# Norm rows summed on DVE before the matmul that reduces them, and activation tables loaded ahead of use

## The chip, the cores and the metric

One NeuronCore of a Trainium2 chip runs the whole program. The metric is the device time of one execution in microseconds (us). Most executions agree within 0.3%. All runs told here are fast (granted TensorE clock 0.998 to 1.0). The engines are PE (matmuls), PEld (its weight loads), DVE (VectorE), ACT (ScalarE), POOL (GpSimd) and SP.

## The reference

Two parts follow each other. Per batch, an attention matrix between channels is made from q and k (6080 rows of 256 channels), with norms over those rows, one per channel; it is applied to v, and the result goes through a two-layer network with a squared ReLU.

```python
qn = q / (np.linalg.norm(q, axis=1, keepdims=True) + 1e-06)
kn = k / (np.linalg.norm(k, axis=1, keepdims=True) + 1e-06)
s = kn.transpose(0, 2, 1) @ qn / tau
s = s - s.max(-1, keepdims=True)
a = np.exp(s)
a /= a.sum(-1, keepdims=True) + 1e-09
x = v @ a                         # 4 batches x 6080 rows x 256
h = x @ w_in                      # 256 -> 2048
r = np.maximum(h, 0.0)
out = (s_moe * (r * r) + b_moe) @ w_out
```

## The kernel before

The kernel walks through 48 groups of 512 tokens (the last has 256), 16 steps each. A step issues two h_ps matmuls and, of the group before, 7 of the 112 small matmuls that make the output from seven products p1 to p7 (a Strassen-like scheme; DVE forms the sums S1 to S4 for it). The products share PSUM tiles, and DVE evicts each one before the next may write there:

```python
products = [
    ("X", G(0, 0), W[:, 0, :, lo], p1),       # evicted to u1
    ("Z", lambda: S[1], T1, p5),              # evicted to u5
    ("X", lambda: S[2], T2, p6),              # waits for u1
    ("Y", G(1, 0), W[:, 1, :, lo], p2),       # Y shares a tile with Z: waits for u5
    ("X", lambda: S[3], T3, p7),
    ("Z", lambda: S[4], W[:, 1, :, hi], p3),
    ("X", G(1, 1), N4, p4),                   # waits for p7's eviction
]                                             # (comments added)
```

Batches 1, 2 and 3 are prepared beside this stream. Their rows come in 12 chunks; per chunk, PE adds to the Gram matrix (s_ps), DVE squares q and ACT squares k, and DVE folds four rows of squares into one row of 2 x 256 (two arrays, q and k). These rows were kept, and reduced over the partitions at the end by matmuls with a column of ones, in a burst:

```python
def fold(half, arrays, last):
    ...
        if last:
            self.rows.append((st["f", half], np_, 1))
...
def add_norms(self, last=False):
    ...
    self.n_ps = x_tile[0][:, 1, : 2 * CH].rearrange("p (a c) -> p a c", a=2)   # unused half of X's tile
    for i, (t, np_, j, a, ch) in enumerate(todo):
        po(nc.tensor.matmul(self.n_ps[:, a, ch : ch + 1], t[:np_, a, j, ts(ch, P)], ones16[:np_, 0:1], ...))

def norms():
    self.add_norms(last=True)
    nrm = sm_pool.tile([P, 2, CH], FP32, tag="nrm", name="nrm")
    po(nc.scalar.activation(out=nrm, in_=self.n_ps, func=AF.Sqrt))
```

The scheduling of a later batch, by steps (cut):

```python
w0 = first_group[b - 1] * FT + (26 if b == 1 else 6)
w1 = first_group[b] * FT - 3
fin_len = 54                       # lead of the finish over the first use
span = (w1 - fin_len) - w0 - 8     # steps over which the chunks are spread
...
for i, f in enumerate(gr.norm_ops(c)):
    at_step(int(sc) + 2 + 1 + i * 3, f)
```

In these traces each engine runs its instructions in the order in which the kernel issues them.

Of the kernel before, what the change touches and what calls it, by code (L numbers as in the profile page):

```python
# [11 lines left out]
AF = mybir.ActivationFunctionType  # L12
# [4 lines left out]
def kernel(  # L17
# [12 lines left out]
    nc = tc.nc  # L30
# [23 lines left out]
    def po(ins):  # L54

        tc.keep_in_program_order(ins)
        return ins
# [30 lines left out]
    def h_tile(name):  # L88
        return ps_h.tile([P, 2, TG], FP32, tag="h_ps", name=name)
# [19 lines left out]
    class Gram:  # L109
# [41 lines left out]
        def norm_ops(self, c):  # L151

            qc, kc = self.tiles[c]
            _, np_, jc = self.chunks[c]
            st = {}

            def squares(a, js):
                def f():
                    if "sq" not in st:
                        st["sq"] = sq_pool.tile([P, 2, JC, C], FP16, tag="sq", name="sq")  # L160
                    if a == 0:
                        po(nc.vector.tensor_mul(  # L162
                            st["sq"][:np_, 0, js, :], qc[:np_, js, :], qc[:np_, js, :]))
                    else:
                        po(nc.scalar.activation(  # L165
                            out=st["sq"][:np_, 1, js, :], in_=kc[:np_, js, :], func=AF.Square))
                return f

            def fold(half, arrays, last):
                def f():  # L170
                    src = st["f", 2 * half] if 2 * half < jc else st["sq"]
                    if ("f", half) not in st:
                        if last:
                            t = f3_pool.tile([P, 2, 1, C], FP16, tag="f3", name="f3")
                        else:
                            t = sq_pool.tile([P, 2, half, C], FP16, tag=f"f{half}", name="f")
                        st["f", half] = t
                    po(nc.vector.tensor_add(  # L178
                        st["f", half][:np_, arrays], src[:np_, arrays, :half, :],
                        src[:np_, arrays, half : 2 * half, :]))  # L180
                    if last:
                        self.rows.append((st["f", half], np_, 1))
                return f

            def unfolded():
                self.rows.append((st["sq"], np_, jc))

            ops = []
            for h in range(0, jc, 4):
                js = slice(h, min(h + 4, jc))  # L190
                ops += [squares(1, js), squares(0, js)]
            if jc == 2:
                return ops + [unfolded]
            if jc == 8:
                ops += [fold(4, slice(0, 1), False), fold(4, slice(1, 2), False)]
            return ops + [fold(2, slice(0, 2), False), fold(1, slice(0, 2), True)]

        def add_norms(self, last=False):

# [15 lines left out]
        def finish_ops(self):  # L215

            st = {}
# [23 lines left out]
                        po(nc.tensor.transpose(  # L241
                            st["t"][:, j, ts(ch, P)], st["s"][:, ch, ts(j, P)], ident32))

            def ready():

                po(nc.scalar.activation(out=warm, in_=ones32[:, 0:1], func=AF.Exp))

            def exps(j):
                if j == 0:
                    st["e"] = sm_pool.tile([P, CH, C], FP16, tag="eT", name="eT")  # L250
                po(nc.scalar.activation(
                    out=st["e"][:, j, :], in_=st["t"][:, j, :], func=AF.Exp,
                    scale=st["r"][:, 0, j : j + 1]))
                if j == 0:
                    self.wa = apool.tile([P, CH, Dff], FP16, tag="wa16", name="wa16")
# [26 lines left out]
            def fold_both(f0, n):  # L282
                def f():

                    two = [self.bank("wa_ps", CH, C)[:, 0, :n], h_tile("wa_ps")[:, 0, :n]]
                    for m in range(CH):
                        fold_mm(f0, n, m, two[m])
                    for m in range(CH):
                        scaled(f0, n, m, two[m])
                return f  # L290
# [8 lines left out]
            if self.b == 0:  # L299

                folds = [fold_both(0, P), fold_both(P, P)]
                folds += [fold_one(2 * P, NW - 2 * P, m) for m in range(CH)]
            else:
                folds = []
            folds += [fold_one(f0, NW, m) for f0 in range(NW if self.b == 0 else 0, Dff, NW)
                      for m in range(CH)]
            return [norms, recip, ready, turn, lambda: exps(0), lambda: exps(1), sums] + folds

        def bank(self, name, a, b):

# [19 lines left out]
    def transpose_v(g):  # L330
        _, nj = group(g)
        v16 = v_tiles.pop(g)
        vT_ps = ps_o.tile([P, CH, TG], FP16, tag="o_ps", name="vT_ps")
        for j in range(nj):
            for ch in range(CH):
                po(nc.tensor.transpose(vT_ps[:, ch, ts(j, P)], v16[:, j, ts(ch, P)], ident16))
        vT = vtpool.tile([P, CH, TG], FP16, tag="vT", name="vT")
        po(nc.vector.tensor_copy(out=vT[:, :, : nj * P], in_=vT_ps[:, :, : nj * P]))
        vT_tiles[g] = vT
# [19 lines left out]
    ones32 = consts.tile([P, P], FP32)  # L359
# [4 lines left out]
    warm = consts.tile([P, 1], FP32)  # L364
# [36 lines left out]
    def keep_busy(n, w, x):  # L401

        idle_ps = h_tile("idle_ps")[:, 0, :]
        for _ in range(n):
            po(nc.tensor.matmul(idle_ps, w, x, start=True, stop=True, skip_group_check=True))

    for c in range(NCH0):
        ops = g0.norm_ops(c)
# [9 lines left out]
            f()  # L418

    fin = g0.finish_ops()  # L420
    fin[0]()
    fin[1]()
    fin[2]()
    keep_busy(5, w_in16[:, 0, :P], w_in16[:, 0, :NW])
    fin[3]()
    transpose_v(0)
    for f in fin[4:11]:
        f()


# [44 lines left out]
    def at_step(s, f):  # L475
        side.setdefault(int(s), []).append(f)


    FIN = (0, 3, 3, 6, 8, 10, 13)
    first_group = [b * N // TG for b in range(B)]  # L480
    for i, f in enumerate(fin[11:]):
        at_step(i // 2 * 4 - 1 + i % 2 if i > 1 else 0, f)
    at_step(14, lambda: po(nc.vector.tensor_scalar_mul(
        out=s_out, in0=s_bc, scalar1=1.0 / (LAM * LAM))))
# [22 lines left out]
    for b in range(1, B):  # L507
        gr = grams[b]
        w0 = first_group[b - 1] * FT + (26 if b == 1 else 6)
        w1 = first_group[b] * FT - 3  # L510
        NCH = len(gr.chunks)
        fin_len = 54
        span = (w1 - fin_len) - w0 - 8
        n = NCH * JC
        for c in range(NCH):
            sc = w0 + span * c * JC / n
            at_step(max(3, sc - 16), lambda gr=gr, c=c: gr.load(c))
            if c == 0:
                at_step(sc, gr.start)
            for j in range(JC):  # L520
                at_step(w0 + span * (c * JC + j) / n, lambda gr=gr, c=c, j=j: gr.mm(c, j))

            def norm_step(gr=gr, c=c, sc=sc):
                ops = gr.norm_ops(c)
                for i, f in enumerate(ops):
                    at_step(int(sc) + 2 + 1 + i * 3, f)
            at_step(sc + 1, norm_step)

        def fin_step(gr=gr, s=w1 - fin_len):
            ops = gr.finish_ops()  # L530
            for i, f in enumerate(ops):
                at_step(int(s) + 1 + (FIN[i] if i < 7 else FIN[6] + 3 + (i - 7) * 3), f)
        at_step(w1 - fin_len, fin_step)


    def segments(g):
# [264 lines left out]
```

## Time and profile before

| | before |
|---|---|
| time, median | 727.7 us (727.43 to 727.76) |
| PE / DVE / ACT busy | 97% / 86% / 75% |
| tiny norm matmuls of batches 1 to 3 | 144, in three bursts of 48 |
| a burst on PE | 1.18 us |
| table load of the square root | 1.28 us, right ahead of it |

Read it from the chain that ended last: it is 89% PE, so PE's issue time and PE's waits decide. The prediction shows those lines and the ones for DVE.

A measure used below: **lost time**. For each matmul I took the time to the start of the next and subtracted the spacing that its width has in an undisturbed stretch of these traces (0.216 us for 512 columns, 0.109 for 256, 0.056 for 128, 0.025 for one); gaps of more than 0.06 us beyond that are added up. (A gap near that limit can fall on either side, so a total is good to about 0.06 us. A time given with a loss is that of the last matmul before the gap.) "Batch 1" runs from the first p1 matmul of group 1 to that of group 8, "batch 2" on to group 20, "batch 3" on to group 32. The chunks of that batch and, except where a run moves it, its finish lie inside. Before, these stretches lasted 106.09, 174.55 and 174.54 us, with 1.16, 0.86 and 0.86 us lost.

### The profile page before, as it was taken

What the parts mean: (1) busy time and instruction counts of PE and PEld (TensorE: products, weight loads), DVE (VectorE), ACT (ScalarE), POOL (GpSimd) and SP (SyncE); (2) the same over time, 40 slices, a digit from 0 to 9 for tenths busy, and PEclk for the clock granted to TensorE, in tenths of its full rate; (3) what the DMA queues carried; (4) which work ended last, traced back from release to release, by engine and by line L of the source; (5) the groups of instructions that cost most, each with busy time, mean ns of one, the idle gap of its engine ahead of it and who ended that gap; (6) DMA issues with size and microseconds to landing.
All of it is one profiled execution on the core that took longest, in us unless ns stands there. A gap on an engine that the chain in (4) does not pass through costs nothing.

```text
span 725.6 us, 17836 instructions
## 1 busy us (share of the span) xinstructions
PE 704.5 (97%) x7618; PEld 509.2 (70%) x7618; DVE 623.6 (86%) x873; ACT 541.5 (75%) x582; POOL 82.4 (11%) x158
## 2 busy tenths in 40 slices
PE   4799999999999999999999999999999999999997
PEld 2556777776777777777677777777668777777776
DVE  4779999988889989988788989998888888888886
ACT  5489877797778777878777778778777777777772
POOL 4522400001111110001010210000000000000000
PEclk9999999999999999999999999999999999999999
DMA  9999993236499754323767685232333333321201
GB/s 237 209 257 143 205 178 75 59 96 125 89 149 163 122 103 89 95 67 76 141 125 127 126 145 126 67 68 65 91 67 78 90 72 73 96 59 51 75 30 75
DMA packets 81600, 79.57 MB, mean 110 GB/s; under 512 B 55696, under 2 KB 56528, under 8 KB 81520
## 3 DMA queue, kind: packets, MB, share of 16 engines
q0 software_dynamic: 21472, 39.46, 32.1%
q1 hardware_dynamic: 59616, 37.64, 20.3%
q8 instruction: 60, 0.98, 0.6%
q10 hardware_dynamic: 432, 1.31, 0.5%
q14 instruction: 20, 0.16, 0.1%
HBM read 78.91 MB, written 24.90 MB: 143 GB/s over the span
## 4 chain that ended last, share of the span: by engine, by line
PE 89%; ACT 4%; DMA 4%; DVE 1%; issue 1%; ACTq 0%; DVEq 0%; POOLq 0%
PE h_ps L566 43%; PE o_ps L710 38%; PE s_ps L142 4%; DMA qk<-in_q_dram 2%; PE wa_ps L278 2%; ACT r L576 2%; DMA raw<-in_q_dram 1%; PE o_ps L614 1%; ACT g L587 1%; ACT sq L165 1%; DVE f L178 0%; ACT L222 0%; PE t_ps L241 0%; ACT T L470 0%; DVE o_sb L594 0%
## 5 line engine op out<-in xcount | busy, mean ns | idle before, releaser
L576 ACT ACTIVATE r<-h_ps 128x1024 f16<-128x1024 f32 (+1 forms) x384 | 387.8, 1013 | 152.3 <-PE h_ps L566 150.7
L566 PE MATMUL h_ps<-vT,wa 128*128 128x512 f16 (+7 forms) x1632 | 451.9, 364 | 0.6 <-ACT r L576 0.4
L710 PEld LDWEIGHTS <-S 128*128 128x128 f16 x2944 | 198.1, 98 | 86.2 <-issue 1.5
L710 PEld LDWEIGHTS <-g 128*128 128x128 f16 x2208 | 155.0, 98 | 74.1
L589 DVE TENSOR_TENSOR g<-r 128x2048 f16<-128x2048 f16 (+2 forms) x154 | 176.4, 1145 | 17.8 <-ACT r L576 17.5
L710 PE MATMUL o_ps<-T,S 128*128 128x128 f16 x2208 | 183.7, 219 | 0.9 <-ACT nrm L222 0.4
L566 PEld LDWEIGHTS <-wa 128*128 128x128 f16 x1632 | 136.1, 98 | 21.6 <-issue 1.0
L710 PE MATMUL o_ps<-w_out,g 128*128 128x128 f16 x1472 | 134.2, 219 | 0.0
L594 DVE SCALAR_TENSOR_TENSOR o_sb<-o_ps,s_out,u 128x256 f32<-128x256 f32 x138 | 66.4, 481 | 51.6 <-PE o_ps L710 49.5
L587 ACT ACTIVATE g<-r 128x1024 f16<-128x1024 f16 x93 | 97.9, 1053 | 0.0
L325 POOL DMA_DIRECT2D v<-in_v_dram x48 | 25.7, 536 | 520.6 <-DMA vT<-v 353.5
L142 PE MATMUL s_ps<-qk 128*128 128x256 f16 (+1 forms) x384 | 69.5, 281 | 14.5 <-ACT qk L133 6.9
L594 DVE SCALAR_TENSOR_TENSOR u<-o_ps,s_out,rowconst 128x256 f32<-128x256 f32 x138 | 65.9, 477 | 2.8 <-PE o_ps L710 1.6
L710 PE MATMUL o_ps<-N,g 128*128 128x128 f16 x736 | 63.5, 219 | 0.0
L710 PE MATMUL o_ps<-w_out,S 128*128 128x128 f16 x736 | 63.4, 219 | 0.0
L165 ACT ACTIVATE sq<-qk 128x1024 f16<-128x1024 f16 (+3 forms) x49 | 50.4, 1033 | 10.6 <-DMA qk<-in_k_dram 7.5
L638 DVE TENSOR_TENSOR S<-S,g 128x2048 f16<-128x2048 f16 (+1 forms) x47 | 56.4, 1201 | 1.3
L636 DVE TENSOR_TENSOR S<-g 128x2048 f16<-128x2048 f16 (+1 forms) x47 | 56.0, 1192 | 0.0
L642 DVE TENSOR_TENSOR S<-g,S 128x2048 f16<-128x2048 f16 x46 | 55.9, 1215 | 0.0
L640 DVE TENSOR_TENSOR S<-g 128x2048 f16<-128x2048 f16 x46 | 55.9, 1214 | 0.0
L142 PEld LDWEIGHTS <-qk 128*128 128x128 f16 (+1 forms) x384 | 32.6, 100 | 19.9 <-DVE qk L132 8.9
L162 DVE TENSOR_TENSOR sq<-qk 128x1024 f16<-128x1024 f16 (+3 forms) x49 | 33.0, 673 | 2.8 <-DMA qk<-in_q_dram 2.8
(68 smaller groups left out, 281.8 us busy)
## 6 DMA issues: line engine op xcount, KB each, us to landing
out_dram<-o_sb SPq DMA_DIRECT2D x46, 512.0 KB, 3.0
v<-in_v_dram POOLq DMA_DIRECT2D x47, 256.0 KB, 3.8
qk<-in_k_dram POOLq DMA_DIRECT2D x42, 256.0 KB, 7.1
qk<-in_q_dram POOLq DMA_DIRECT2D x42, 256.0 KB, 7.8
vT<-v SPq DMA_TRANSPOSE x182, 2.8
w<-in_moe_w_out_dram POOLq DMA_DIRECT2D x4, 512.0 KB, 12.2
raw<-in_q_dram ACTq DMA_DIRECT2D x2, 512.0 KB, 6.5
raw<-in_k_dram SPq DMA_DIRECT2D x2, 512.0 KB, 6.8
```

What stands on the lines that cost most here:

```text
L142: po(nc.tensor.matmul(self.s_ps[:, ch, :], kc[:np_, j, ts(ch, P)], qc[:np_, j, :], start=(c == 0 and j == 0 and ch == 0), stop=(c == len(s ...
L165: po(nc.scalar.activation(out=st["sq"][:np_, 1, js, :], in_=kc[:np_, js, :], func=AF.Square))
L566: po(nc.tensor.matmul(dst, wa[:, ci, ts(m, P)], src, start=(ci == 0), stop=(ci == CH - 1), skip_group_check=True))
L576: po(nc.scalar.activation(out=r16[:, :, i % 2, :n], in_=h_tiles.pop((g, i))[:, :, :n], func=AF.Relu))
L587: po(nc.scalar.activation(out=dst, in_=src, func=AF.Square))
L589: po(nc.vector.tensor_mul(dst, src, src))
L594: po(nc.vector.scalar_tensor_tensor(out=dst, in0=src, scalar=s_out, op0=ALU.mult, in1=add, op1=ALU.add))
L636: po(nc.vector.tensor_add(T[1], A21, A22))
L638: po(nc.vector.tensor_sub(T[2], T[1], A11))
L640: po(nc.vector.tensor_sub(T[3], A11, A21))
L642: po(nc.vector.tensor_sub(T[4], A12, T[2]))
L710: po(nc.tensor.matmul(st[name][:, j, :], a()[:, i, ts(j, P)], w[:, i, :], start=first, stop=last, skip_group_check=True))
```

## The change

The intent is to take most of the tiny matmuls off PE: the rows of chunks 2 to 12 are added onto the first chunk's row on DVE, so that a burst has 4 matmuls. And the square root's table is to be in place when the norms are: a dummy activation loads it 12 steps ahead, as one already did for the exponential.

```diff
-                    if last:
+                    if last and (self.b == 0 or c == 0):
                         self.rows.append((st["f", half], np_, 1))
...
+            def into_first():
+                dst, src = self.rows[0][0][:np_], st["f", 1][:np_]
+                po(nc.vector.tensor_add(dst, dst, src))
...
-            return ops + [fold(2, slice(0, 2), False), fold(1, slice(0, 2), True)]
+            ops += [fold(2, slice(0, 2), False), fold(1, slice(0, 2), True)]
+            return ops + [into_first] if self.b > 0 and c > 0 else ops
...
-            def ready():
-                po(nc.scalar.activation(out=warm, in_=ones32[:, 0:1], func=AF.Exp))
+            def ready(func):
+                po(nc.scalar.activation(out=warm, in_=ones32[:, 0:1], func=func))
...
-            return [norms, recip, ready, turn, ...] + folds
+            return [lambda: ready(AF.Sqrt), norms, recip, lambda: ready(AF.Exp), turn, ...] + folds
...
-    FIN = (0, 3, 3, 6, 8, 10, 13)
+    FIN = (-12, 0, 3, 3, 6, 8, 10, 13)
...
-        span = (w1 - fin_len) - w0 - 8
+        span = (w1 - fin_len) - w0 - 12
```

The last line squeezes the chunks into 81 steps in place of 85 for batch 1, and 117 in place of 121 for the others, as a chunk now has five operations three steps apart.

More of the change, by code (lines that the diff above doesn't have):

```diff
@@ L306, in finish_ops @@
                       for m in range(CH)]
-            return [norms, recip, ready, turn, lambda: exps(0), lambda: exps(1), sums] + folds
+            return [lambda: ready(AF.Sqrt), norms, recip, lambda: ready(AF.Exp), turn, lambda: exps(0), lambda: exps(1), sums] + folds
         def bank(self, name, a, b):
@@ L420 @@
     fin = g0.finish_ops()
-    fin[0]()
     fin[1]()
     fin[2]()
+    fin[3]()
     keep_busy(5, w_in16[:, 0, :P], w_in16[:, 0, :NW])
-    fin[3]()
+    fin[4]()
     transpose_v(0)
-    for f in fin[4:11]:
+    for f in fin[5:12]:
         f()
@@ L476, in at_step @@
         side.setdefault(int(s), []).append(f)
-    FIN = (0, 3, 3, 6, 8, 10, 13)
+    FIN = (-12, 0, 3, 3, 6, 8, 10, 13)
     first_group = [b * N // TG for b in range(B)]
-    for i, f in enumerate(fin[11:]):
+    for i, f in enumerate(fin[12:]):
         at_step(i // 2 * 4 - 1 + i % 2 if i > 1 else 0, f)
@@ L531, in fin_step @@
             for i, f in enumerate(ops):
-                at_step(int(s) + 1 + (FIN[i] if i < 7 else FIN[6] + 3 + (i - 7) * 3), f)
-        at_step(w1 - fin_len, fin_step)
+                at_step(int(s) + 1 + (FIN[i] if i < 8 else FIN[7] + 3 + (i - 8) * 3), f)
+        at_step(w1 - fin_len - 12, fin_step)
     def segments(g):
```

## The prediction

> **What bounds the kernel now.** I read the page first (busy shares, then the chain that ended last), then the instructions of line 211, which the change thins out, then the chain and the timeline around one burst of them, and last the DVE, which gets the new work.
>
> The page's first part and the two summary lines of its chain:
>
> ```profile
> PE 704.5 (97%) x7618; PEld 509.2 (70%) x7618; DVE 623.6 (86%) x873; ACT 541.5 (75%) x582; POOL 82.4 (11%) x158
> PE 89%; ACT 4%; DMA 4%; DVE 1%; issue 1%; ACTq 0%; DVEq 0%; POOLq 0%
> PE h_ps L566 43%; PE o_ps L710 38%; PE s_ps L142 4%; DMA qk<-in_q_dram 2%; PE wa_ps L278 2%; ACT r L576 2%; DMA raw<-in_q_dram 1%; PE o_ps L614 1%; ACT g L587 1%; ACT sq L165 1%; DVE f L178 0%; ACT L222 0%; PE t_ps L241 0%; ACT T L470 0%; DVE o_sb L594 0%
> ```
>
> The kernel is a stream of matmuls: 89% of the chain is PE, and the granted clock is full in all 40 slices. So an instruction taken off PE after the first 36 us shortens the run by its issue time, unless what stands beside it cannot follow. DVE, at 86%, is the engine that might not.
>
> The norms of a later batch (1, 2, 3) are made by one burst of tiny matmuls in the middle of that stream. The chain in order of time around batch 1's burst:
>
> ```profile
> 148.56 0.39 PE o_ps L710 x7
> 148.95 1.18 PE o_ps L211 x48
> 150.13 0.45 PE h_ps L566 x2
> ```
>
> 48 matmuls hold PE for 1.18 us, 24.6 ns each from start to start. The 163 ns that the list of line 211 gives for one is latency, which overlaps. Around batch 2's burst the chain reads
>
> ```profile
> 322.47 1.02 ACT r L576
> 323.49 0.02 issue
> 323.51 1.28 ACT L222
> 324.79 0.01 issue
> 324.80 0.18 ACT nrm L222
> 324.99 0.04 issue
> 325.03 0.55 PE o_ps L710 x7
> ```
>
> Here the end of the burst is not what lets PE go on: the square root waits for its table (1.28 us), and the next product into the same PSUM tile waits for the square root's read. In the timeline the weight stream restarts at 325.03, while the pair of h_ps matmuls before it began at 324.26 and needs 0.43: the restart would have been at 324.69, so 0.34 us are lost. The gap between the same starts is the same in batch 3; batch 1 loses 0.08.
>
> For DVE, the groups that matter, and the busy time in the three stretches in which a later batch's Gram matrix is gathered:
>
> ```profile
> L178 DVE TENSOR_TENSOR f<-f 128x512 f16<-128x512 f16 (+1 forms) x47 | 19.7, 419 | 0.4
> L636 DVE TENSOR_TENSOR S<-g 128x2048 f16<-128x2048 f16 (+1 forms) x47 | 56.0, 1192 | 0.0
> ...
> 66.00:147.00 81.00, 80.55 (x854) 58.69 (x852) 77.53 (x111) 65.18 (x75) 11.76 (x22) 1.00 0.71 135
> 184.00:322.00 138.00, 137.98 (x1516) 100.80 (x1514) 124.20 (x172) 105.02 (x109) 15.92 (x30) 1.00 0.61 114
> 376.00:497.00 121.00, 120.98 (x1330) 89.41 (x1328) 110.42 (x154) 93.01 (x97) 11.67 (x22) 1.00 0.58 113
> ```
>
> The columns after the length are PE, PEld, DVE, ACT, POOL. DVE is busy 95.7% of batch 1's stretch (3.5 us idle) and 90 to 91% of the other two (13.8 and 10.6 us idle).
>
> **What the Trainium skill says.** "TensorE: Matmul & The Clock Gate", section "Wait — 56ns, not 53.3ns?": start-to-start never drops below about 25 ns however small N is. The trace agrees: 24.6 ns at N=1. "VectorE: DVE Perf Modes", section "The perf-mode tier table": a 16-bit tensor_tensor of 2048 elements takes 1224 ns, at most the 2x mode; the trace has 1192 to 1215 for such adds. "ScalarE: Activation LUTs", section "What ACT_TABLE_LOAD costs": about 1283 ns plus a drain of about 1380. The trace has the 1283, but no further 1380 after it: the square root above starts 0.01 us after its table load ends. I use 1.28.
>
> **The change part by part.**
>
> Removed from PE: a later batch has 12 chunks, each leaving one row of 2 arrays x 2 halves, so 48 matmuls with their weight loads. With the rows added onto the first one, 4 remain. 44 x 24.6 ns = 1.08 us a batch, and all of it lies on the path: 3 x 1.08 = 3.24 us. Batch 0 is untouched (the new fold is for b > 0, and its list of operations only shifts its indices by one).
>
> Moved on ACT: the square root's table now comes with a dummy activation 12 steps (about 10 us) earlier; the load of the exponential was already separate. The number of loads stays the same, and 3 dummies of 0.20 us are added. At the new place ACT has room: between 312 and 318 us relus of 1.02 us follow each other at 1.65 us, so 0.62 idle in each period, and the built order puts the load between pairs of relus with no square in the next four. The load and dummy take 1.40 us from start to the next relu (that is what the exponential's took, 153.37 to 154.77), so that relu is about 0.8 us late. By the timeline a relu ends about 0.8 to 1.0 us before PE writes its buffer again, and the exponential's own load stopped no h_ps matmul. I count no loss, 0.1 at most for one batch.
>
> What that frees: after a burst of about 0.1 us, the next X product stands 0.1 + 0.43 us behind the burst's start. The square root now waits only for the relu in front of it on ACT. With batch 2's times that relu ends at 323.49, the root would end at about 323.65, and PE would want the tile at 323.04 + 0.10 + 0.43 = 323.57: a wait of about 0.05 to 0.15 instead of 0.34. I count 0.25 for each of batches 2 and 3 and 0.05 for batch 1: 0.55 us.
>
> Added on DVE: 11 adds a batch of the form 128x512, 33 in all. One lasts 0.42 us, but the next DVE instruction starts 0.33 after it (73.63 to 73.96 in the timeline), so 11 x 0.33 = 3.7 us a batch. In batches 2 and 3 that fits into the idle 13.8 and 10.6 us. In batch 1 it meets 3.5 us of idle time. There the gathering is also squeezed from 85 steps to 81, so the same adds come 5% closer together, which PE partly shares, its Gram matmuls coming closer too. The limit is reached there, so I walked the built order of DVE from one wait for PE to the next. In the before trace each group of 16 steps (about 15 us) has 0.5 to 1.2 us of DVE idle in its last third. The added work is 0.35 (first group), 0.7, 1.6, 0.7 and 0.7 us in the five groups. The lateness at the third output eviction comes out as 0, 0, 0.3, 0.7 and 0.4 us. PE feels that through the first sum S of each group (line 636), whose first matmul starts only 0.06 to 0.8 us after it is ready. In the new order the small adds fall less often right ahead of it, and only the last group comes out short, by about 0.1. I allow 0.3 us for batch 1, as such a walk can miss one of five, and 0.3 for batches 2 and 3 together, for sums that shift by one add and for PE's waits on a relu, which move with the steps.
>
> Sum: 727.7 - 3.24 - 0.55 + 0.3 + 0.3 = 724.5 us, 0.44% faster.
>
> **The rivals.** First, DVE becomes the bound of batch 1. For it: 95.7% busy, 3.7 us to add into 3.5 us of idle, and a first sum that in one group (at 145.8) is ready just when it is used. Against it: idle time at waits for PE shows that DVE is resynchronised each group, and the stretch without Gram work that follows (DVE 86% busy) pays lateness back. Were all idle time unusable, batch 1 would lose up to about 2 us and the time would be 726.5. Second, the moved table load stalls PE instead of the square root: relus late by 0.8 us with 0.8 to 1.0 of slack could cost 0.2 to 0.5 us in each batch, giving 725.5. Third, the burst was hidden anyway: DVE and ACT used it to catch up, so that PE waits elsewhere for what it no longer spends there. For it: the chain passes through DVE for 5.8 us just ahead of batch 1's burst (142.02 to 147.80), so DVE is behind there. Against it: right after the burst the chain is PE alone, and the sums have 0.4 us of slack with no Gram work left. If half the 3.24 were given back the time would be 726.1.
>
> **The range and the chances.** The best case is all of the 3.24 and of the roots' 0.76, with no loss: 723.7, or a little less if the shifted schedule also drops some of the small waits of before (0.17 us four times on a relu in batches 2 and 3). The rivals reach 725.5 to 726.5 each, and two of them together 727. Eight in ten: 723.4 to 726.4. 2% is 14.6 us; nothing in the change reaches that either way, short of a surprise in a state of the chip or a table loaded many more times, and the built order shows no such loads.
>
> **What would show it.** The list of the tiny matmuls should have 12 in place of 144 on o_ps, each burst about 0.1 us in the chain. The square root should start less than 0.2 us after the relu before it with no table load between. The waits for nrm on PE should fall to 0.1 or vanish. DVE busy should rise by 33 x 0.42, to about 637 us (88%), with batch 1's stretch near 99%. PE's waits on S and on relus should stay within half a microsecond of before. It would be wrong if the matmuls after the burst stand apart by waits on DVE (line 642 of the new kernel), or if h_ps matmuls wait for a relu just after the new table load.

## The result, and the profile after

The changed kernel takes 725.05 us (724.96 to 725.23, 4 runs) against 727.62 for the kernel before in the same rounds: 2.57 us or 0.35% less. The ratio given with the run is 0.9965, 95% interval 0.9948 to 0.9982. Such ratios are the mean time of one kernel's fast runs over that of the other's of the same rounds, so not quite the ratio of the medians quoted. The time lies inside the predicted range, 0.55 us above the predicted 724.5.

The page's first part and the engines of its chain, kernel after:

```profile
PE 702.4 (97%) x7486; PEld 506.5 (70%) x7486; DVE 634.1 (88%) x906; ACT 542.4 (75%) x585; POOL 82.8 (11%) x158
...
PE 83%; DVE 9%; DMA 5%; ACT 1%; issue 1%; POOL 1%; ACTq 0%; POOLq 0%
```

132 matmuls are gone from PE, and DVE is 10.5 us busier. DVE now has 9% of the chain, against 1% before. Most of that lies between 60 and 150 us, in and around batch 1's stretch.

The chain around batch 2's burst, kernel after:

```profile
322.91 0.39 PE o_ps L716 x7
323.30 0.08 PE o_ps L217 x4
323.38 0.45 PE h_ps L572 x2
323.83 0.41 PE o_ps L716 x7
```

Before, this was a chain through ACT's table load and square root. Now PE follows on PE: the burst is 0.08 us, and the next X product starts on time. What ACT does there, from its timeline, kernel after:

```profile
322.55 1.02 ACT L582 ACTIVATE r<-h_ps 128x1024 f16<-128x1024 f32 x1
323.45 0.18 ACT L228 ACTIVATE nrm<-o_ps 128x4 f32<-128x4 f32 x1
```

The square root starts 0.90 us after the start of the relu ahead of it, with no table load between, and ends at 323.63, before PE wants the tile at 323.83. PE's waits for nrm are gone from the list of waits.

The group of the new adds among the groups by line, kernel after:

```profile
L188 DVE TENSOR_TENSOR f<-f,f 128x512 f16<-128x512 f16 (+1 forms) x33 | 13.9, 420 | 0.0
```

And the busy time in the same three stretches as before (columns PE, PEld, DVE, ACT, POOL), kernel after:

```profile
66.00:147.00 81.00, 79.74 (x839) 57.84 (x837) 79.88 (x121) 65.33 (x74) 11.72 (x22) 1.00 0.72 131
184.00:322.00 138.00, 137.82 (x1512) 100.59 (x1510) 127.60 (x183) 106.46 (x111) 14.33 (x27) 1.00 0.56 113
376.00:497.00 121.00, 120.82 (x1323) 89.05 (x1322) 113.66 (x165) 95.07 (x100) 11.66 (x22) 1.00 0.55 111
```

In batch 1's stretch DVE is busy 98.6% of the time and PE's busy time fell from 80.55 to 79.74: PE waits there. In the other two DVE is at 92 to 94%.

The lengths of the three stretches settle where the 2.5 us came from:

| us | before | after | difference | lost time before / after |
|---|---|---|---|---|
| batch 1 | 106.09 | 105.96 | -0.13 | 1.16 / 2.24 |
| batch 2 | 174.55 | 173.36 | -1.19 | 0.86 / 0.74 |
| batch 3 | 174.54 | 173.36 | -1.18 | 0.86 / 0.74 |

Each batch saves 44 x 24.6 ns = 1.08 us of burst. Batch 1 gives all but 0.1 of that back as waits. The new ones are at 74.5 (0.49 us), 103.5 (0.38), 136.4 (0.22) and 142.5 (0.52); two of before, 0.32 at 78.3 and 0.22 at 147.5, are gone. The first of them in the timeline, kernel before and then kernel after:

```profile
73.96 0.48 DVE L594 SCALAR_TENSOR_TENSOR u<-o_ps,s_out,rowconst 128x256 f32<-128x256 f32 x1
74.36 0.68 DVE L162 TENSOR_TENSOR sq<-qk 128x1024 f16<-128x1024 f16 x1
```

```profile
73.94 0.69 DVE L162 TENSOR_TENSOR sq<-qk 128x1024 f16<-128x1024 f16 x1
...
74.54 0.48 DVE L600 SCALAR_TENSOR_TENSOR u<-o_ps,s_out,rowconst 128x256 f32<-128x256 f32 x1
...
75.07 0.22 PE L716 MATMUL o_ps<-w_out,g 128*128 128x128 f16 x1 [0.33 <-DVE u L600]
```

Before, the eviction to u5 ran at 73.96 and the squares after it. In the squeezed schedule the squares fall ahead of the eviction, it ends at 75.02, and p2's first matmul, which writes the same tile, waits for it. No new add is involved in this wait (the first one starts at 81.1): the order moved. Run 3, without the squeeze, does not have it.

### The profile page after: what moved, and what is told of

The parts are those of the page before. It is cut to its first block, busy times and chain, and to the rows that moved or that the text cites. A ratio compares the mean times of both kernels' runs of the same rounds, so it can differ in the third digit from the quotient of the medians.

```text
span 723.1 us, 17605 instructions
## 1 busy us (share of the span) xinstructions
PE 702.4 (97%) x7486; PEld 506.5 (70%) x7486; DVE 634.1 (88%) x906; ACT 542.4 (75%) x585; POOL 82.8 (11%) x158
## 4 chain that ended last, share of the span: by engine, by line
PE 83%; DVE 9%; DMA 5%; ACT 1%; issue 1%; POOL 1%; ACTq 0%; POOLq 0%
PE h_ps L572 40%; PE o_ps L716 36%; PE s_ps L142 3%; PE wa_ps L284 2%; DMA qk<-in_q_dram 2%; DMA w_in<-in_moe_w_in_dram 1%; DVE f L178 1%; DMA qk<-in_k_dram 1%; DVE o_sb L600 1%; DVE S L644 1%; DVE S L642 1%; DVE g L595 1%; ACT r L582 1%; DVE sq L162 1%; PE o_ps L620 1%
```

## The experiments

All results are correct against the reference, and each was timed against the kernel before, whose median was 727.42 to 727.68 in all of them. Lost time is given for batches 1, 2 and 3.

| run | median us | ratio (95% interval) | lost time us |
|---|---|---|---|
| before | 727.62 | | 1.16, 0.86, 0.86 |
| the change | 725.05 | 0.9965 (0.9948 to 0.9982) | 2.24, 0.74, 0.74 |
| table only | 726.99 | 0.9992 (0.9979 to 1.0004) | 1.28, 0.52, 0.52 |
| adds only | 729.40 | 1.0025 (1.0012 to 1.0039) | 3.68, 2.18, 2.24 |
| no squeeze | 724.96 | 0.9965 (0.9952 to 0.9977) | 2.45, 0.54, 0.60 |
| batch 1 keeps its burst | 725.15 | 0.9966 (0.9954 to 0.9979) | 1.23, 0.74, 0.74 |
| finish 12 steps later | 725.38 | 0.9967 (0.9954 to 0.9979) | 1.71, 1.05, 1.10 |
| adds on POOL | 728.60 | 1.0012 (1.0000 to 1.0025) | 4.20, 1.62, 1.36 |
| adds twice | 733.51 | 1.0079 (1.0065 to 1.0092) | 6.36, 2.91, 2.91 |
| finish 16 steps later | 725.03 | 0.9963 (0.9951 to 0.9976) | 3.07, 0.24, 0.24 |
| the same, batch 1 alone | 725.99 | 0.9977 (0.9964 to 0.9991) | 3.07, 0.75, 0.75 |
| adds at step 15 | 724.21 | 0.9955 (0.9942 to 0.9967) | 2.34, 0.29, 0.29 |
| adds at step 6 | 730.73 | 1.0043 (1.0029 to 1.0057) | 4.34, 2.48, 2.46 |
| step 15, batch 1 later | 723.94 | 0.9949 (0.9935 to 0.9962) | 1.78, 0.29, 0.29 |

**1. The table's move alone**

```diff
 (the changed kernel)
-  if last and (self.b == 0 or c == 0):
+  if last:                                   # all rows kept, bursts of 48
-  return ops + [into_first] if self.b > 0 and c > 0 else ops
+  return ops
-  span = (w1 - fin_len) - w0 - 12
+  span = (w1 - fin_len) - w0 - 8
```

> Only the table's move, bursts of 48 kept, no adds. My theory: the wait for the square root's table (0.34 us in batches 2 and 3, 0.08 in batch 1 of the kernel before) goes, nothing else changes: 726.9 us (0.7 below the kernel before). Rival A, the moved load costs what it saves, as relus come late: 727.6 or more. Rival B, the table is the larger part of the gain: under 726.2.

726.99 us, as expected. The lost time of batches 2 and 3 falls by 0.34 us each, the wait for the square root, and no h_ps matmul waits behind the moved load. Rivals A and B fall. The interval reaches past 1, so the time alone would not settle it; the trace's stretches do (batch 2: 174.55 to 174.20 us).

**2. The adds alone**

```diff
 (the kernel before; no dummy for the square root)
-  if last:
+  if last and (self.b == 0 or c == 0):
+  def into_first():                          # as in the change
-  return ops + [fold(2, slice(0, 2), False), fold(1, slice(0, 2), True)]
+  ops += [fold(2, slice(0, 2), False), fold(1, slice(0, 2), True)]
+  return ops + [into_first] if self.b > 0 and c > 0 else ops
-  span = (w1 - fin_len) - w0 - 8
+  span = (w1 - fin_len) - w0 - 12
```

> Only the adds (and the 81-step squeeze), the square root's table still loaded right ahead of it. My theory: the table load, which starts at the end of the relu whether the burst is long or short, now sets when PE goes on; the burst's 1.08 us a batch turn into a wait of about the same length for nrm, and batch 1's wait for DVE evictions (about 1 us) comes on top: 728.4 to 729.1 us, slower than before. Rival, the two parts simply add up: 725.7 us.

729.40 us, slower than before, and a little more so than my range. The chain around batch 2's burst in this run:

```profile
324.18 1.02 ACT r L582
325.21 0.02 issue
325.22 0.29 ACT L228
325.52 1.00 issue
326.52 0.18 ACT nrm L228
326.70 0.04 issue
326.74 0.55 PE o_ps L716 x7
```

And its list of waits:

```profile
PE o_ps L716 <- ACT nrm L228: 3.8, 3, 1.3
```

The relu ends, the table load follows (part of it shown as issue), the square root, and then PE may go on. This path is as long with a short burst as with a long one. The lost time at this place is 1.44 us in each batch, so the 1.08 us saved turn into a wait. The two parts do not add up: the table's move alone gives 0.6, the adds alone -1.8, and both together 2.6.

**3. The squeeze taken back**

```diff
-  span = (w1 - fin_len) - w0 - 12
+  span = (w1 - fin_len) - w0 - 8
```

> The changed kernel with the gathering spread over 85 steps in batch 1 again (121 in place of 117 in the others). If batch 1 is bound by how much DVE work falls into a step, 5% less dense gathering gives back part of its loss: 724.5 us, PE's waits on DVE in batch 1 at 1.2 us in place of 1.9. Rival, only the order counts (which add stands just ahead of which eviction): a change of up to 0.5 us either way, with waits at other places.

724.96 us, the same as with the squeeze. Batch 1 lost no less (2.45 us), but at other places: 105.2, 118.6, 142.4, and 0.48 us at 149.6, where the norms' matmuls waited for the last add. Batches 2 and 3 lost 0.14 to 0.2 less. My expectation failed for batch 1; the outcome is the one that the rival, order, foretold.

**4. Batch 1 with its burst**

```diff
-  if last and (self.b == 0 or c == 0):
+  if last and (self.b <= 1 or c == 0):
-  return ops + [into_first] if self.b > 0 and c > 0 else ops
+  return ops + [into_first] if self.b > 1 and c > 0 else ops
-  span = (w1 - fin_len) - w0 - 12
+  span = (w1 - fin_len) - w0 - (8 if b == 1 else 12)
```

> The changed kernel, but batch 1 keeps its 48 matmuls and has no adds and 85 steps. My theory now: batch 1's adds gave back what its shorter burst saved, so this changes nothing: 725.0 us (724.7 to 725.3), with batch 1's waits on DVE back at 1.2 us and its burst at 1.18. Rival (the prediction on record): batch 1's adds cost 0.3 and save 1.1, so this is 725.8 us.

725.15 us, as expected: undoing the change in batch 1 costs 0.1 us, less than the spread of the runs. Its stretch takes 106.03 us with 48 matmuls and 105.96 with 4. In batch 1 the adds pay for nothing; the gain of the change is batches 2 and 3.

**5. The finish 12 steps later**

```diff
-  fin_len = 54
+  fin_len = 42
```

> The changed kernel with the finish of each later batch moved 12 steps nearer to where its weights are used (54 steps of lead become 42), so that batch 1's chunks are gathered over 93 steps in place of 81. If batch 1 is bound by DVE throughput, 15% less dense gathering takes most of its 1.9 us of waits away: 724.0 us (723.6 to 724.5), and batches 2 and 3 stay. Rival, as the run over 85 steps suggests, the place of single instructions counts more than the density: 724.7 to 725.3.

725.38 us, a miss. Batch 1's waits on DVE between 75 and 147 us did go. But the finish now falls on another place of the group, and each batch loses 0.54 us at the square root. The chain there in this run:

```profile
157.62 1.02 ACT r L582
158.65 0.29 ACT g L593
158.94 0.55 issue
159.49 0.17 ACT nrm L228
159.66 0.04 issue
159.70 0.55 PE o_ps L716 x7
```

An ACT square (g, 1.05 us) stands between the relu and the square root (one, not the two of which a later expectation speaks). Batch 1 lost 0.5 us less than with the change, and batches 2 and 3 lost 0.3 to 0.4 more each.

**6. The adds on POOL**

```diff
-  po(nc.vector.tensor_add(dst, dst, src))
+  po(nc.gpsimd.tensor_add(dst, dst, src))
```

> The changed kernel with the 33 adds on GpSimd, which is 11% busy. If the waits of batch 1 come from the adds' time on DVE alone, they go back to the 1.2 us of before: 724.1 us (723.7 to 724.5), DVE busy back at 624 us. Rivals: GpSimd takes its adds in order with its loads, and the norms' matmuls then wait for the last one (PE waits on POOL at the burst, 725 us or more); or the adds slow DVE's own instructions (mean of the 128x2048 adds above 1.22 us).

728.60 us. The second rival holds; of the first there is no sign, as no norm matmul waits for POOL. An add takes a median of 1.47 us on POOL (0.42 on DVE), and DVE's own large operations get longer: its busy time, expected back at 624 us, was 639.0. DVE's largest group with shapes kept apart, kernel after and then this run:

```profile
L595 DVE TENSOR_TENSOR g<-r 128x2048 f16<-128x2048 f16 x137 | 167.0, 1219 | 11.7 <-ACT r L582 11.5
```

```profile
L595 DVE TENSOR_TENSOR g<-r 128x2048 f16<-128x2048 f16 x137 | 176.0, 1285 | 11.5 <-ACT r L582 11.3
```

The Trainium skill says, in "GPSIMD Engine Reference", section "1. Specifications", that POOL's SBUF interface is shared with VectorE and contended by DVE instructions with two SBUF inputs. These are such instructions, and the trace agrees: the 19 of the 137 that ran beside one of the adds took 1.71 us on average (2.07 at most), the other 118 took 1.22. The evictions, which read one operand from PSUM, took 0.48 us beside an add as elsewhere.

**7. Each add twice**

```diff
   po(nc.vector.tensor_add(dst, dst, src))
+  po(nc.vector.tensor_add(src, src, src))    # useless, same form
```

> The changed kernel with a second, useless add of the same form after each of the 33. If DVE throughput bounds batch 1, its 11 extra adds of 0.33 us show nearly whole there, +3 to +3.7 us, and batches 2 and 3, with over 7 us of DVE idle left each, add under 0.7 each: 728.3 to 729.8 us. If only the place of single instructions counts, the extra is under 1.2 us in all: under 726.3 us.

733.51 us, outside my range. Batch 1 loses 4.1 us more than with the change, over what I expected, so extra DVE time shows there in full: DVE is at 99% of its stretch. Batches 2 and 3 lose 2.2 us more each, where I had allowed 0.7, although DVE still has 6 to 9 us of idle time in their stretches. So idle time on DVE is not free time, even there.

**8 and 9. The finish 16 steps later, in all batches and in batch 1 alone**

```diff
-  fin_len = 54
+  fin_len = 38                        # run 9: 38 if b == 1 else 54
```

> The changed kernel with 38 steps of lead in place of 54: 16 steps, one whole group, later, so that the norms fall on the same place in a group as before, and the gathering has 97 steps in batch 1 (133 in the others). In the run with 42 steps batch 1's waits on DVE mostly went, but the square root fell behind two ACT squares and PE waited 0.54 us for it in each batch. If that reading is right, both waits are gone here: 723.6 us (723.2 to 724.1). Rival, whatever is saved ahead of the burst comes back behind it, since the finish then meets the start of the next batch: 724.7 to 725.4.

> The same for batch 1 alone. It keeps batches 2 and 3 as they are in the changed kernel, so it isolates batch 1: if its loss was DVE density, 723.9 us (723.5 to 724.3), with batch 1's waits on DVE after 75 us under 0.5 us in place of 1.6. Rival as in the run for all batches: 725.0.

725.03 and 725.99 us; both missed for batch 1. (Run 8's time lies in its rival's range, but not for the rival's reason: the losses stand ahead of the finish, not behind it.) Sixteen steps keep the finish at the same place in a group, and in batches 2 and 3 (run 8) the lost time falls to 0.24 us each, with no wait at the square root. But batch 1 lost 3.07 us although DVE had more room (77.98 us busy in the 81 us stretch, run 9): 97 steps over 12 chunks are 8.1 steps a chunk, two chunks to a group, so the small operations fall on the same places in every group, among them just ahead of p2's eviction. PE lost 0.34 us at it in each of four groups (94.1, 109.3, 124.6 and 139.8) and 0.71 at 154.7. Each time DVE ran an add, the sum S4, a fold and then the eviction; at 79, where the add is missing from this row, PE lost 0.06 us. "Density" alone was the wrong theory.

**10 and 11. The same adds, at a chosen step of the group**

```diff
   for i, f in enumerate(ops):
-      at_step(int(sc) + 2 + 1 + i * 3, f)
+      s = int(sc) + 2 + 1 + i * 3
+      if i == 4 and s + (15 - s) % FT <= w1 - fin_len:      # run 11: 6
+          s += (15 - s) % FT
+      at_step(s, f)
```

> The changed kernel, same 81 steps, same 33 adds, but each add is held back to the next step 15 of a group (unless the finish comes first), where DVE stands between the evictions of the products p7 and p3 and mostly waits for PE. If what costs is an add standing just ahead of an eviction that PE waits for, batch 1's waits on DVE fall from 1.9 us after 74 us to under 1.0, batches 2 and 3 lose 0.2 less each: 723.8 us (723.3 to 724.3). Rival, DVE throughput alone: the adds cost the same wherever they stand, 724.8 to 725.3.

> The same with step 6, right after the sum S3 and ahead of the eviction of p5, which the product p2 waits for. If place counts, PE waits for that eviction (u) in nearly each group of each gathering: 726.3 us (725.6 to 727.5), waits on DVE u in batch 1 over 1.5 us. Rival, throughput alone: 724.8 to 725.3 like the other.

724.21 and 730.73 us: the same 33 adds, in the same 81 and 117 steps, 6.5 us apart. At step 6 they stand ahead of the eviction that p2 waits for. The waits of PE on that eviction from 60 to 720 us, kernel after, step 15, step 6:

```profile
PE o_ps L716 <- DVE u L600: 0.9, 4, 0.3
```

```profile
PE o_ps L719 <- DVE u L603: 0.3, 1, 0.3
```

```profile
PE o_ps L719 <- DVE u L603: 4.8, 9, 1.0
```

Place counts, then, and more than I had expected of step 6. But at step 15 the gain is in batches 2 and 3 (0.45 us each). Batch 1 still lost 2.34 us, 1.7 of it after 74 us (1.6 with the change) where I expected under 1.0, with DVE 98.7% busy. In batch 1 the right place is not enough.

**12. Room and place together**

```diff
 (run 10)
-  fin_len = 54
+  fin_len = 38 if b == 1 else 54
```

> Both at once for batch 1: its finish 16 steps later, so that its chunks spread over 97 steps, and the adds of all batches held back to step 15. Alone, the first was slower (adds fell ahead of the same eviction in every group) and the second left batch 1's waits where they were (DVE 98.7% busy there). If batch 1 needs both room and the right place, its waits on DVE after 74 us fall from 1.7 to under 0.6: 723.2 us (722.8 to 723.6). Rival, more room does not help batch 1 at all: 724.0 to 725.0.

723.94 us, the lowest of all, but between my range and the rival's. Between 80 and 145 us batch 1 now loses nothing; 0.85 us are lost in group 1, 0.26 at 147.7, and 0.54 at 153.8 where p3 waits for p2's eviction. My edit has a flaw that bears on the last: the limit reads `fin_len` after the loop over batches has ended, when it is 54 again, so batch 1's last three adds were not held back, and one of them stands in the same row as in run 9 (add at 151.84, S4, fold, eviction at 153.90). What a clean version would take was not run. Batch 1's lost time of 1.78 us is the smallest of the runs that have adds in batch 1 except run 5 (1.71, with 0.54 of it at the square root).

## Why the prediction was right or wrong

**The bound, right.** PE's issue time set the end, and 44 matmuls a batch were worth 1.08 us wherever DVE could follow: batches 2 and 3 shortened by 1.19 and 1.18 us, and the prediction's terms for them (1.08 + 0.25 - 0.15) give 1.18.

**The table, right, with a size off and a link missed.** The wait for nrm vanished where I expected 0.05 to 0.15 to be left: 0.34 us a batch (run 1) for my 0.25. The moved load stopped no relu that PE needed. But the prediction wrote the burst's 3.24 us and the root's 0.55 as two savings that add. Run 2 shows that the first needs the second: the chain that the prediction itself quoted around 325 has no piece of the burst in it, and without the table's move the adds save nothing.

**Batch 1, the step that failed.** "I allow 0.3 us for batch 1" was the mis-sized term: it lost 1.08 us more than before (2.24 against 1.16). The walk along DVE's order took the first sum S as the place where PE feels lateness; the new waits of the trace are on the evictions of p5, p1 and p7, all ahead of the burst. One of them (0.49 us at 74.5) has no add before it, only the squares of a chunk that the squeeze moved ahead of it. So the first rival held in kind, DVE as the bound of batch 1, with 1.08 us where it allowed about 2.

**Batches 2 and 3, a smaller miss.** I allowed 0.15 us of loss in each. Leaving out the root's 0.34 us, they lost 0.52 before and 0.74 after, so 0.22. The root's gain was larger by 0.09, and the two errors cancel: that the terms add up to 1.18 is luck. DVE's busy time rose by 10.5 us, not by the 33 x 0.42 = 13.9 I wrote, as neighbouring instructions overlap; 33 x 0.33 = 10.9 was the fitting figure. (A reading to correct: the 1192 ns that I gave for sums of 2048 elements is the mean of a group with a smaller form in it; with shapes kept apart the four sums take 1214 to 1224 ns.)

**The other rivals.** The second, a stall by the moved load, is excluded by run 1 and by the trace. The third, a burst hidden anyway because DVE caught up behind it, is not borne out: batches 2 and 3 kept their saving, and batch 1's new waits (74.5 to 142.5) all stand ahead of its burst at 149.8, none behind it. Run 4 shows only that burst and adds cost the same in batch 1.

**What stays open.** That batch 1 needs both room and place on DVE is the reading that fits runs 5, 7, 9, 10 and 12, but it is not fully shown: run 12, which had both but for its flaw, missed its range and still lost 1.78 us (1.16 before). How the 1.08 us split between DVE's load and its order was not separated, since every shift of the schedule changes both; the squeeze without the adds was not run. Nor was it tested why doubling the adds costs 2.2 us in batches 2 and 3, where a single set at step 15 costs almost nothing; run 11 makes their place the likely reason.

## What to carry to other kernels

When two waits end at the same instruction, removing the shorter one gives nothing, and the gain of a pair of edits has to be tried as a pair. Idle time of a second engine is only worth what its position allows: small work put in front of an eviction that the bound engine waits for can cost most of its time (at step 6, batches 2 and 3 lost 2.2 us more each than at step 15, of 11 x 0.33 = 3.6 us), and the same work at a better step was nearly free there (0.29 us lost in all). So before moving work onto an engine, look at which instruction of it the bound engine waits for next, and put the work after that one.

## What the Trainium skill lacked or had wrong

- "ScalarE: Activation LUTs", section "What ACT_TABLE_LOAD costs": it adds a drain of about 1380 ns to the load's 1283 ns. In these traces the next activation starts 0.01 us after the load's end (323.51 + 1.28, then 324.80).
- "GPSIMD Engine Reference", section "3.1 Elementwise — side-by-side cycle accounting", gives about 2.6 cycles per element for an add of two tensors, from which an estimate for 512 elements at its 1.2 GHz is 1.11 us, but no figure for an add beside a busy DVE. The runs show a 16-bit add of 128x512 at 1.14 to 2.61 us (the profile of POOL is rough), median 1.47, 3.5 times DVE's 0.42.
- No page that I read says how a wait for an ACT table can hide the cost of a matmul burst that ends earlier; here 1.08 us of burst were worth nothing until the table was moved (729.40 against 725.05 us).
